# Attention and two expert stages on one core: a list scheduler with measured durations, a cost for changes of tile size, and constants fetched first

## The chip, the core and the metric

The kernel runs on one core of a Trainium2 chip. The metric is the device time of one execution in microseconds (us); lower is better. A core has five instruction streams that run side by side and wait for each other through semaphores: TensorE (PE, with its weight loads shown as PEld), VectorE (DVE), ScalarE (ACT), GpSimd (POOL) and SyncE (SP), which here issues all DMAs.

## What is computed

Float32 attention with a soft cap on the scores feeds a first expert stage, whose activation is a ratio of two polynomials, and a second one that takes the largest of three products:

```python
scores = cap * np.tanh((q @ k.T / sqrt(64)) / cap)          # 2 x 12 heads, 448 tokens, 64 wide
attn = softmax(scores); x = attn @ v                        # -> 896 tokens x 768
h = x @ w_in                                                # 768 -> 2048
P = a0 + a1*h + a2*h**2 + a3*h**3
Q = 1 + |b0|*|h| + |b1|*h**2
x = (P / (Q + 1e-6)) @ w_out                                # 2048 -> 768
y = max(x @ w1, x @ w2, x @ w3) @ w_out2                    # 768 -> 768
```

The weights arrive as 64-bit numbers and are decoded on the chip. Every product of the expert stages is made of three matmuls (high by high, high by low, low by high parts), so that float32 accuracy is kept.

## The kernel before

**Stages.** Attention goes by 6 groups `d` of 4 heads. For each, `scores(d, i)` (lines 481 to 519) makes 7 tiles of scores; ACT turns each into weights with a tanh (L512) and an exp (L515), both on 128x896. `weighted_rest` and `weighted` (L532, L551) multiply them with v, `summed` (L574) adds up the rows, and the sums go through DRAM and back to be spread over the partitions (`sums`, `comp`, `rsum`, `row`), after which x is scaled and split (L610 to L618). Then come 32 units `up(n)`, a 128-wide slice `fc` of w_in by one of two batches `b` each, of 18 matmuls of 128x448 (L638); two units make a pair `k`. ACT and DVE turn a pair's product into the ratio: abs and cubic read the PSUM bank on ACT (L655, L658), first and second on DVE (L669, L672), linear (L662, L664) and denom (L677) make the denominator, Ln and Exp on ACT (L693, L694) and newton, numer, refine on DVE (L697, L700, L703) the quotient, and L717, L720 split it into `gh` and `gl`. `down("oa", ...)` (L745) multiplies a pair with the first half of w_out's columns into six accumulators, 18 matmuls a pair; `down("ob", ...)` does the other half once all pairs are there. `branches` (L836) and `output` (L895) are the second expert stage. Between them runs the decoding of 56 weight blocks (L378 to L408), five passes over 128x768 and a subtraction, mostly on DVE.

**Order.** No engine's order is written by hand. `Flow.add` records each step with the engines that can do it and a duration for each; `Flow.issue` (lines 147 to 261) then simulates the core with these numbers, gives each free engine the ready step of least due time that fits into free slots and banks, and emits it. PE steps get due times from a running clock that is started at 6.0 (line 361); all others from their users. `place` picks PSUM banks: `av` values go to banks 4 and 5, `h` values to 6 and 7 while scores are still to come, and any of the 8 after that, the one that has been free longest. `port` (lines 135 to 145) refuses POOL a step where DVE will soon do one that shares its port with POOL.

**Waits.** The pools are opened with `reuse_waits="tile"`: a reader or writer of a tile waits for the accesses of that tile before it. The PSUM tiles `b0` to `b3` are two banks each (line 293), so that both banks of one tile share their waits. There are 12 matmuls of warm-up (`3 * WARM`, L358) on a zeroed tile at the start.

Of the kernel before, what the change touches and what calls it, by code (L numbers as in the profile page):

```python
# [18 lines left out]
P = 128  # L19
# [15 lines left out]
NFULL = S // P  # L35
WARM = 4
EARLY = 4

AHEAD, NEAR, LEAVE = 200.0, 30.0, 4

LATE, KEEP = 40.0, 4

SHARE = 0.5
# [10 lines left out]
class Op:  # L54
    def __init__(self, engines, after, vals, fn, shared, due, leave, ahead, size):
        self.engines, self.after, self.vals, self.fn = engines, after, vals, fn
        self.shared, self.due, self.leave, self.ahead, self.size = shared, due, leave, ahead, size
        self.next, self.soft, self.left, self.ready, self.done, self.on = [], [], 0, 0.0, None, None

# [5 lines left out]
class Flow:  # L65
# [10 lines left out]

    def add(self, engines, fn, after=(), vals=(), shared=False, due=None, leave=0, ahead=1e9, size=0.0):
        first = next(iter(engines))
        if first == "pe":
            due = self.clock  # L80
            self.clock += engines["pe"]
        after = [a for a in after if a is not None]
        op = Op(engines, after, list(dict.fromkeys(vals)), fn, shared, due, leave, ahead, size)
# [50 lines left out]

    def port(self, t, op, ready, busy, current):

        if busy["dve"] > t + 1e-9 and current["dve"].shared:
            return False
        room = max(0.0, busy["dve"] - t)
        for o in ready:  # L140
            if "dve" in o.engines and o is not op and o.ready <= t + 1e-9:
                if o.shared:
                    return room >= SHARE * op.engines["pool"]
                room += o.engines["dve"]
        return True

    def issue(self):
        ops = self.ops
        for op in reversed(ops):
            d = min(op.engines.values())  # L150
# [7 lines left out]
        busy = dict.fromkeys(names, 0.0)  # L158
        current = dict.fromkeys(names)
        wire, head, left = 0.0, 0, len(ops)  # L160
        ready, events, seq = [], [], 0
# [5 lines left out]
        while left:  # L167
# [4 lines left out]
            while moved:  # L172
                moved = False
                for e in names:
                    if busy[e] > t + 1e-9:
                        continue
                    blocked = set()
                    ahead = dict.fromkeys(names, 0.0)
                    for op in ready:
                        first = next(iter(op.engines))  # L180
                        cost = op.engines[first]
# [13 lines left out]
                        if op.shared and e == "dve" and busy["pool"] > t + 1e-9:  # L195
                            continue
                        if e == "pool" and not self.port(t, op, ready, busy, current):
                            continue
                        if e != first and op.engines[e] > max(0.0, busy[first] - t) + ahead[first] + cost:
                            ahead[first] += cost  # L200
                            continue
                        break
                    else:
                        continue
                    ready.remove(op)
                    for v in op.vals:
                        if v.at is None:
                            self.take(v)
                    dur = op.engines[e]
                    op.on = e  # L210
                    current[e] = op
# [57 lines left out]
def attention_moe(ctx: ExitStack, tc: tile.TileContext, qk, v, w_in, w_out, w123, w_out2, par, out):  # L269
# [53 lines left out]

    con_in = dma(lambda: con, lambda: par.broadcast_to([P, 8]), size=0.004, issue=0.3)
    idle = slot("idle", F32R)
# [33 lines left out]

    add({"pe": 2.4}, warm_up, [zero], [idle, warm])  # L360
    fl.clock = 6.0

# [118 lines left out]
    def scores(d, i):  # L481
# [13 lines left out]
        def ends(e):  # L495
# [9 lines left out]
        done = add(  # L505
            {"pe": 0.8}, products if whole_ else ends, [QK[pi][1] for pi in pis], [QK[pi][0] for pi in pis] + [t]
        )
# [8 lines left out]

        th = add({"act": 0.80}, soft, [done, scale_in], [t, x])
        last_tanh.append(th)
# [5 lines left out]
    def weighted_rest(d):  # L524
# [11 lines left out]

        done = add({"pe": 0.85}, products, [ex, got_v], [*o, x, vr])
        AV[d] = o, done
# [4 lines left out]
    def weighted(d, r):  # L543
        vr, got_v = VV[d]
        o, dep = AV[d][0][r], AV[d][1]
        for n in range(NFULL):
# [8 lines left out]

            dep = add({"pe": 0.76}, products, [ex, got_v, dep], [o, x, vr])
        xu, parts = XU[d]
# [4 lines left out]
    def summed(d):  # L562
        t, row, dep = Val("av", f"sm{d}"), Val("row", f"sr{d}"), None
        for n in range(NFULL + 1):
# [13 lines left out]

            dep = add({"pe": 0.76}, products, [x[1] for x in xs] + [filled, dep], [t] + [x[0] for x in xs])
        got = add(  # L580
# [44 lines left out]
    def up(n):  # L625
# [4 lines left out]
        for part in range(3):  # L630

            def products(e, part=part):
# [10 lines left out]
            dep = add(  # L643
                {"pe": 1.2}, products, [w.done, dep] + [x[1] for x in xs], [h, w.hi, w.lo] + [x[0] for x in xs],
            )
# [82 lines left out]
    def down(which, n, half):  # L728
# [4 lines left out]
        for o in range(3):  # L733
# [14 lines left out]

            users.append(add({"pe": 0.6}, products, [w.done, h_, l_], [a, w.hi, w.lo, hi, lo]))
            if half and len(users) == 1:  # L750
# [69 lines left out]
    def branches(oc, b):  # L820
# [6 lines left out]
        for lo, hi in ranges:  # L827
            for m in range(3):
                w, o = weights["m", oc, m], outs[m]

                def products(e, w=w, o=o, lo=lo, hi=hi):
# [7 lines left out]
                last[m] = add(  # L839
                    {"pe": 0.6 * (hi - lo)}, products, [w.done, last[m]] + [x[1] for x in xs],  # L840
                    [o, w.hi, w.lo] + [x[0] for x in xs],
# [37 lines left out]
    def output(t):  # L879
# [4 lines left out]
        for half in range(2):  # L884
# [3 lines left out]
            def products(e, o=o, ck=ck):  # L888
# [9 lines left out]
            done = add(  # L898
                {"pe": 18 * 0.171}, products, [w.done for w in ws] + [d for h in H3 for d in h[2]],
                [o] + [x for w in ws for x in (w.hi, w.lo)] + [x for h in H3 for x in h[:2]],  # L900
# [65 lines left out]
```

## Time and profile before

| | |
|---|---|
| three runs | 557.7, 554.9, 557.12 us; median 557.12 |
| profiled execution | 559.87 us |
| its span | 558.1 us |
| mean granted TensorE clock | 0.985 |
| busy PE / DVE / ACT / POOL | 521.8 / 355.5 / 289.5 / 56.7 us |
| matmuls recorded | 2640 |
| DMA | 58.36 MB, mean 105 GB/s |

The profiled execution is 2.75 us above the median of the runs. Busy times are averages over stages with different limits; the section of rows below cuts the span into stages. In a row of the timeline the columns are start, length, engine, line, operation, out<-in with partitions x elements and count, and in brackets the idle time before it and what ended it.

### The profile page before, as it was taken

To read this page: it belongs to the slowest core of one execution; us is meant where nothing else is said; L and a number is where in the kernel's file an instruction comes from. 1 tells how busy PE (TensorE), PEld (TensorE's weight loads), DVE (VectorE), ACT (ScalarE), POOL (GpSimd) and SP (SyncE) were. 2 spreads that over 40 slices of the span, in tenths; PEclk is the share of its full clock that TensorE was granted. 3 is DMA by queue.
4 is the path that set the end of the run, shared out by engine and by line. 5 is a ranking of instruction groups with operands and counts; after the bars stand their busy time and mean duration, and the time that the engine had idled before them with its cause. 6 is when DMAs were issued, how large, how long until landed. Compare 5 with 4: busy or idle time off the path is not lost.

```text
span 558.1 us, 6678 instructions
## 1 busy us (share of the span) xinstructions
PE 521.8 (93%) x2640; PEld 415.0 (74%) x2640; DVE 355.5 (64%) x490; ACT 289.5 (52%) x365; POOL 56.7 (10%) x52
## 2 busy tenths in 40 slices
PE   7999999899986988788789999999999999999996
PEld 4222224468875878677678999999999999999996
DVE  0326798789897878787678989998895236112000
ACT  4999888665776657454348774535362111001111
POOL 0210021100321221120121100002000000000000
PEclk9999999999997999899799999999999999999999
DMA  7692455425210001302010457785550000000121
GB/s 288 253 358 72 158 160 159 137 91 168 93 58 1 0 1 56 115 17 98 0 56 1 127 160 265 253 281 200 189 166 1 1 1 0 1 0 1 58 84 58
DMA packets 16447, 58.36 MB, mean 105 GB/s; under 512 B 3592, under 2 KB 6944, under 8 KB 16416
## 3 DMA queue, kind: packets, MB, share of 16 engines
q1 hardware_dynamic: 16416, 57.94, 30.5%
q8 instruction: 20, 0.33, 0.2%
q14 instruction: 11, 0.09, 0.1%
HBM read 55.10 MB, written 2.84 MB: 104 GB/s over the span
## 4 chain that ended last, share of the span: by engine, by line
PE 75%; DVE 11%; ACT 6%; DMA 4%; issue 1%; SPq 1%; ACTq 0%; DVEq 0%
PE b L836 24%; PE b L638 17%; PE b L745 14%; PE b L895 8%; PE b L493 4%; PE b L551 4%; PE b L574 3%; DVE W L669 3%; ACT W L658 3%; DVE W L672 3%; DMA row<-rsum 2%; ACT A L655 2%; DMA con<-in_par_dram 1%; SPq L321 1%; PE b L532 1%
## 5 line engine op out<-in xcount | busy, mean ns | idle before, releaser
L638 PE MATMUL b<-x,whin 128*128 128x448 f32 x384 | 114.9, 381 | 20.9 <-DVE W L672 16.9
L836 PE MATMUL b<-x,whm 128*128 128x448 f32 x432 | 122.7, 365 | 0.0
L638 PEld LDWEIGHTS b<-x,whin 128*128 128x128 f32 x384 | 72.8, 194 | 39.0 <-DVE W L672 18.9
L836 PEld LDWEIGHTS b<-x,whm 128*128 128x128 f32 x432 | 81.2, 188 | 6.4
L836 PE MATMUL b<-x,wlm 128*128 128x448 f32 x216 | 78.9, 365 | 0.0
L638 PE MATMUL b<-x,wlin 128*128 128x448 f32 x192 | 71.8, 374 | 0.0
L658 ACT ACTIVATE W<-b,con 128x448 f32<-128x448 f32 x32 | 22.8, 724 | 39.4 <-PE b L638 35.0
L512 ACT ACTIVATE e<-b,qscale 128x896 f32<-128x896 f32 x42 | 41.0, 1019 | 4.4 <-PE b L493 4.3
L836 PEld LDWEIGHTS b<-x,wlm 128*128 128x128 f32 x216 | 40.6, 188 | 3.2
L515 ACT ACTIVATE e<-e,con 128x896 f32<-128x896 f32 x42 | 42.0, 1050 | 0.0
L745 PE MATMUL b<-gl,whoa 128*128 128x448 f32 x96 | 36.4, 379 | 3.6 <-DVE gl L720 3.6
L638 PEld LDWEIGHTS b<-x,wlin 128*128 128x128 f32 x192 | 37.2, 194 | 3.2
L864 ACT CAST h3h<-t 128x448 fp32r<-128x448 f32 x9 | 5.1, 567 | 65.7 <-DVE t L859 65.7
L745 PE MATMUL b<-gh,whoa 128*128 128x448 f32 x96 | 36.1, 376 | 2.5 <-ACT gh L717 2.5
L669 DVE TENSOR_TENSOR W<-b,W 128x448 f32<-128x448 f32 x32 | 19.7, 622 | 27.4 <-ACT A L655 16.6
L493 PE MATMUL b<-qk 64*128 64x448 f32 x144 | 35.3, 583 | 2.0 <-ACT e L512 2.0
L745 PE MATMUL b<-gh,wloa 128*128 128x448 f32 x96 | 35.9, 374 | 0.0
L745 PE MATMUL b<-gh,whob 128*128 128x448 f32 x96 | 35.2, 366 | 0.0
L745 PE MATMUL b<-gh,wlob 128*128 128x448 f32 x96 | 35.1, 365 | 0.0
L745 PE MATMUL b<-gl,whob 128*128 128x448 f32 x96 | 35.1, 365 | 0.0
L677 POOL TENSOR_TENSOR T<-T,A 128x448 f32<-128x448 f32 x15 | 20.5, 1369 | 102.7 <-ACT T L662 75.6
L551 PE MATMUL b<-e,v 128*64 128x448 f32 x144 | 30.7, 551 | 0.0
(114 smaller groups left out, 905.3 us busy)
## 6 DMA issues: line engine op xcount, KB each, us to landing
raw<-in_w_out_dram SPq DMA_DIRECT2D x22, 768.0 KB, 4.2
raw<-in_w_dram SPq DMA_DIRECT2D x18, 768.0 KB, 4.4
raw<-in_w_in_dram SPq DMA_DIRECT2D x16, 768.0 KB, 5.7
qk<-in_qk_dram SPq DMA_DIRECT2D x12, 448.0 KB, 5.1
v<-in_v_dram SPq DMA_DIRECT2D x6, 448.0 KB, 8.6
row<-rsum SPq DMA_DIRECT2D x24, 112.0 KB, 3.5
out_dram<-ob SPq DMA_DIRECT2D x6, 384.0 KB, 2.8
out_dram<-ob SPq DMA_DIRECT2D x2, 192.0 KB
```

The costliest lines, as they stand in the source:

```text
L493: pe.matmul(pair(t)[:, j, :S], k[rr], q[rr], start=True, stop=True)
L512: act.activation(two(x), pair(t)[:, :, :S], AF.Tanh, scale=qscale)
L515: act.activation(two(x), two(x), AF.Exp, scale=cap)
L551: pe.matmul(bank(o)[j * D : j * D + D, :S], whole(vr, n, r, j), two(x)[:, j], start=False, stop=n == NFULL - 1,)
L574: pe.matmul(bank(t)[g, :S], ones[:, 0 if n < NFULL else 1 + r], two(xs[r][0])[:, j], start=n == 0, stop=n == NFULL, tile_position=(0, (2 * ...
L638: pe.matmul(bank(h)[:, :S], w_, x_, start=cc == 0 and i == 0, stop=cc == NCC - 1 and i == len(terms) - 1)
L658: act.activation(two(w_)[:, i], bank(h)[:, :S], AF.Identity, bias=a2, scale=a3)
L669: dve.tensor_tensor(out=two(w_)[:, i], in0=bank(h)[:, :S], in1=two(w_)[:, i], op=ALU.mult)
L677: engine[e].tensor_tensor(out=two(t_)[:, i], in0=two(t_)[:, i], in1=two(a_)[:, i], op=ALU.mult)
L745: pe.matmul(bank(a)[:, :S], w_, g_, start=count[half, o, b] == 1, stop=count[half, o, b] == 3 * NFC)
L836: pe.matmul(bank(o)[:, :S], w_, x_, start=cc == 0 and i == 0, stop=cc == NCC - 1 and i == 2)
L895: pe.matmul(bank(o)[:, :NH], h_, w_, start=i == 0, stop=i == len(terms) - 1)
```

## The change

The durations that the scheduler plans with are altered: a score, weighting or sum step on PE from 0.76 to 0.85 to `FULL` = 0.752, an up step from 1.2 to 6 x 0.203, a down step from 0.6 to 3 x 0.203, an output step from 18 x 0.171 to 18 x 0.1733, a tanh from 0.80 to 0.89, the warm-up from 2.4 to 3.6. Each PE step of the attention now has a `mode` (its tile shape), a change of mode costs `SWITCH` = 0.1 in the plan, and PE may take a later ready step of its present mode if that is due at most `SAME` = 3.0 after the first one. `port` no longer counts DVE steps that are held back for lack of slots or for being too early. SP holds back a transfer that is due more than 14.0 ahead while the planned wire is over 2.0 behind. The constants get a due time of -20, so that they are fetched first; the warm-up falls from 12 to 9 matmuls and the clock of due times starts at 4.5.

```diff
-WARM = 4
+WARM = 3
+BACKLOG = 14.0, 2.0
+SWITCH, SAME = 0.1, 3.0
+MM, MO, FULL = 0.203, 0.1733, 0.752
...
     def port(self, t, op, ready, busy, current, v0):
...
             if "dve" in o.engines and o is not op and o.ready <= t + 1e-9:
+                if not (o.due - v0 < o.ahead and self.fits(o, v0)):
+                    continue
...
+                    choice = None
                     for op in ready:
+                        if choice and (op.due > choice.due + SAME or "pe" not in op.engines or op.mode != mode):
+                            continue
...
+                        if e == "sp" and op.due - v0 > BACKLOG[0] and wire > t + BACKLOG[1]:
+                            continue
...
+                        if e == "pe" and SAME and op.mode != mode:
+                            choice = choice or op
+                            continue
+                        choice = op
                         break
...
                     dur = op.engines[e]
+                    if e == "pe":
+                        dur += SWITCH if mode != op.mode else 0.0
+                        mode = op.mode
...
-    con_in = dma(lambda: con, lambda: par.broadcast_to([P, 8]), size=0.004, issue=0.3)
+    con_in = dma(lambda: con, lambda: par.broadcast_to([P, 8]), size=0.004, issue=0.45, due=-20.0)
...
-    add({"pe": 2.4}, warm_up, [zero], [idle, warm])
-    fl.clock = 6.0
+    add({"pe": 3 * WARM * 0.4}, warm_up, [zero], [idle, warm])
+    fl.clock = 4.5
...
-            {"pe": 0.8}, products if whole_ else ends, [QK[pi][1] for pi in pis], [QK[pi][0] for pi in pis] + [t]
+            {"pe": FULL}, products if whole_ else ends, [QK[pi][1] for pi in pis], [QK[pi][0] for pi in pis] + [t],
+            mode="rows" if whole_ else "both",
...
-        th = add({"act": 0.80}, soft, [done, scale_in], [t, x])
+        th = add({"act": 0.89}, soft, [done, scale_in], [t, x])
...
-        done = add({"pe": 0.85}, products, [ex, got_v], [*o, x, vr])
+        done = add({"pe": FULL}, products, [ex, got_v], [*o, x, vr], mode="both")
...
-            dep = add({"pe": 0.76}, products, [ex, got_v, dep], [o, x, vr])
+            dep = add({"pe": FULL}, products, [ex, got_v, dep], [o, x, vr], mode="halves")
...
-                {"pe": 1.2}, products, [w.done, dep] + [x[1] for x in xs], [h, w.hi, w.lo] + [x[0] for x in xs],
+                {"pe": 6 * MM}, products, [w.done, dep] + [x[1] for x in xs], [h, w.hi, w.lo] + [x[0] for x in xs],
...
-            users.append(add({"pe": 0.6}, products, [w.done, h_, l_], [a, w.hi, w.lo, hi, lo]))
+            users.append(add({"pe": 3 * MM}, products, [w.done, h_, l_], [a, w.hi, w.lo, hi, lo]))
```

The lines of the new file are 22 to 25 higher: L321 becomes L343, L638 L663, L658 L683, L655 L680, L669 L694, L672 L697, L677 L702, L703 L728, L720 L745, L745 L770.

Since the planner's numbers decide every order, the order of the program moves almost everywhere. Three places matter below. The first is SP at the program's start (`con` is the constants, `qk` and `v` the attention's inputs by pair and group, `raw` the undecoded weights). Before:

```order
L321 DMA qk0_110<-in_qk_dram 128x896
L321 DMA qk1_112<-in_qk_dram 128x896
L321 DMA con_68<-in_par_dram 128x8
L321 DMA qk2_127<-in_qk_dram 128x896
L321 DMA qk3_129<-in_qk_dram 128x896
L321 DMA v0_131<-in_v_dram 128x896
L321 DMA qk4_133<-in_qk_dram 128x896
```

and now:

```order
L343 DMA con_68<-in_par_dram 128x8
L343 DMA qk0_111<-in_qk_dram 128x896
L343 DMA qk1_122<-in_qk_dram 128x896
L343 DMA qk2_124<-in_qk_dram 128x896
L343 DMA qk3_126<-in_qk_dram 128x896
L343 DMA v0_145<-in_v_dram 128x896
L343 DMA qk4_155<-in_qk_dram 128x896
```

The constants go ahead of the first two `qk`, and the first transfers of weights fall behind `v2`.

The second is PE around the end of the up pair `fc` = 13 and the start of the down steps of pair 10 (`b0` to `b3` are PSUM tiles, `x` the scaled attention result of batch and chunk, `whin` and `wlin` the parts of w_in, `whoa` and `wloa` those of w_out, `gh` and `gl` the parts of the activation). Before:

```order
L638 MATMUL b3_84<-x0_5_668,whin13_1566 128x448 x2
L638 MATMUL b3_84<-x0_5_668,wlin13_1585 128x448
L638 MATMUL b3_84<-x1_4_1037,whin13_1566 128x448 x2
L638 MATMUL b3_84<-x1_4_1037,wlin13_1585 128x448
L638 MATMUL b3_84<-x1_5_1046,whin13_1566 128x448 x2
L638 MATMUL b3_84<-x1_5_1046,wlin13_1585 128x448
L745 MATMUL b2_83<-gh10_1779,whoa5_1680 128x448 [waits Activation_49]
L745 MATMUL b2_83<-gl10_1797,whoa5_1680 128x448
L745 MATMUL b2_83<-gh10_1779,wloa5_1723 128x448
L745 MATMUL b2_83<-gh10_1779,whoa5_1680 128x448
L745 MATMUL b2_83<-gl10_1797,whoa5_1680 128x448
L745 MATMUL b2_83<-gh10_1779,wloa5_1723 128x448
```

and now:

```order
L663 MATMUL b3_84<-x0_5_646,whin13_1764 128x448 x2
L663 MATMUL b3_84<-x0_5_646,wlin13_1772 128x448
L663 MATMUL b0_81<-x1_4_1035,whin13_1764 128x448 x2
L663 MATMUL b0_81<-x1_4_1035,wlin13_1772 128x448
L663 MATMUL b0_81<-x1_5_1046,whin13_1764 128x448 x2
L663 MATMUL b0_81<-x1_5_1046,wlin13_1772 128x448
L770 MATMUL b2_83<-gh10_1781,whoa5_1839 128x448
L770 MATMUL b2_83<-gl10_1802,whoa5_1839 128x448
L770 MATMUL b2_83<-gh10_1781,wloa5_1842 128x448
L770 MATMUL b0_81<-gh10_1781,whoa5_1839 128x448 [waits Activation_49]
L770 MATMUL b0_81<-gl10_1802,whoa5_1839 128x448
L770 MATMUL b0_81<-gh10_1781,wloa5_1842 128x448
```

Both units of a pair were in the two banks of `b3`; now the first is in `b3` and the second in `b0`, each beside an accumulator of the down steps, and the second group of three down matmuls waits for ACT. At the end of the same 18 down matmuls there is now a wait for DVE ahead of the group in `b3`:

```order
L770 MATMUL b1_82<-gh10_1781,whoa5_1839 128x448
L770 MATMUL b1_82<-gl10_1802,whoa5_1839 128x448
L770 MATMUL b1_82<-gh10_1781,wloa5_1842 128x448
L770 MATMUL b3_84<-gh10_1781,whoa5_1839 128x448 [waits DVE_49]
L770 MATMUL b3_84<-gl10_1802,whoa5_1839 128x448
L770 MATMUL b3_84<-gh10_1781,wloa5_1842 128x448
L663 MATMUL b3_84<-x0_0_430,whin14_1850 128x448 x2
```

Before, the first wait for DVE stood at the first matmul of the next up pair, behind all 18.

The third is DVE at the last pair (`W15`, `T15`) and the activation of pair 14 (`dec`, `wl`, `wh` are blocks of weights in decoding). Before:

```order
L664 TENSOR_SCALAR T15_2122<-A15_2115,absb_69 128x448
L720 TENSOR_TENSOR gl14_2131<-W14_2015,gh14_2110 128x896
L677 TENSOR_TENSOR T15_2122<-T15_2122,A15_2115 128x448 x2
L669 TENSOR_TENSOR W15_2129<-b3_84,W15_2129 128x448 x2
L672 SCALAR_TENSOR_TENSOR W15_2129<-W15_2129,con_68,b3_84 128x448 x2
L393 SCALAR_TENSOR_TENSOR decob1_2079<-raw1_75,decob1_2079 128x768
L384 TENSOR_SCALAR decob2_2088<-decob2_2088 128x768
L419 CAST whob1_2182<-decob1_2079 128x768
L403 SCALAR_TENSOR_TENSOR decob2_2088<-raw2_76,decob2_2088 128x768
L697 SCALAR_TENSOR_TENSOR T15_2122<-T15_2122,qone_72,A15_2115 128x896
L700 SCALAR_TENSOR_TENSOR W15_2129<-W15_2129,con_68,A15_2115 128x896
L408 TENSOR_TENSOR wlob1_2202<-decob1_2079,whob1_2182 128x768
```

and now:

```order
L689 TENSOR_SCALAR T15_2115<-A15_2111,absb_69 128x448
L406 TENSOR_SCALAR decob1_2089<-decob1_2089 128x768
L702 TENSOR_TENSOR T15_2115<-T15_2115,A15_2111 128x448
L694 TENSOR_TENSOR W15_2113<-b3_84,W15_2113 128x448
L689 TENSOR_SCALAR T15_2115<-A15_2111,absb_69 128x448
L745 TENSOR_TENSOR gl14_2138<-W14_2021,gh14_2120 128x896
L702 TENSOR_TENSOR T15_2115<-T15_2115,A15_2111 128x448
L694 TENSOR_TENSOR W15_2113<-b0_81,W15_2113 128x448
L697 SCALAR_TENSOR_TENSOR W15_2113<-W15_2113,con_68,b3_84 128x448
L697 SCALAR_TENSOR_TENSOR W15_2113<-W15_2113,con_68,b0_81 128x448
L415 SCALAR_TENSOR_TENSOR decob1_2089<-raw1_75,decob1_2089 128x768
L722 SCALAR_TENSOR_TENSOR T15_2115<-T15_2115,qone_72,A15_2111 128x896
```

The low part of pair 14 (`gl14`) stood ahead of pair 15's first and second; now it stands between them, and the four readers of the banks go in the order first, first, second, second, by bank.

## Rows read from the trace of the kernel before

**Rows 1.** Windows: window, length, busy us (count) by engine, granted clock, DMA share, GB/s.

```profile
14.00:56.00 42.00, 42.00 (x246) 11.49 (x246) 17.69 (x24) 40.94 (x46) 6.62 (x7) 1.00 0.61 227
56.00:98.00 42.00, 40.71 (x244) 13.01 (x240) 35.26 (x58) 36.72 (x41) 5.43 (x5) 1.00 0.51 159
101.00:171.20 70.20, 61.76 (x315) 48.14 (x311) 61.37 (x86) 46.78 (x63) 12.85 (x10) 0.99 0.31 100
171.20:320.30 149.10, 130.53 (x596) 116.33 (x597) 118.91 (x149) 86.13 (x112) 26.54 (x17) 0.95 0.13 44
305.20:558.10 252.90, 248.26 (x1261) 232.81 (x1259) 136.09 (x192) 82.56 (x109) 6.21 (x4) 1.00 0.30 102
```

**Rows 2.** Timeline of PE and ACT over the first 15 us.

```profile
1.38 4.61 PE L358 MATMUL b<-idle 128*128 128x448 f32 x12 [1.38 <-DVE idle L326]
5.91 1.77 PE L493 MATMUL b<-qk 64*128 64x448 f32 x8
10.58 3.72 PE L493 MATMUL b<-qk 64*128 64x448 f32 x16 [1.98 <-ACT e L512]
...
9.52 6.40 ACT L512 ACTIVATE e<-b,qscale 128x896 f32<-128x896 f32 x7
```

**Rows 3.** The chain that ended last, in order of time: start, length, what.

```profile
1.64 7.40 DMA con<-in_par_dram
...
25.22 0.90 PE b L551 x4
...
53.16 4.66 PE b L551 x24
...
187.28 7.58 PE b L638 x36
...
297.84 7.53 PE b L638 x36
```

**Rows 4.** Timeline of PE: a matmul that waited in the loop of up and down.

```profile
171.23 0.74 PE L745 MATMUL b<-gl,whoa 128*128 128x448 f32 x1 [3.10 <-DVE gl L720]
```

**Rows 5.** Window right behind this wait.

```profile
171.20:174.00 2.80, 2.77 (x7) 2.48 (x8) 2.01 (x3) 2.11 (x4) 1.59 (x1) 0.50 0.00 0
```

**Rows 6.** Timeline of one handover from an up pair to the next.

```profile
206.05 0.36 PE L638 MATMUL b<-x,wlin 128*128 128x448 f32 x1
...
206.53 1.15 DVE L697 SCALAR_TENSOR_TENSOR T<-T,qone,A 128x896 f32<-128x896 f32 x1
...
207.26 0.36 PE L638 MATMUL b<-x,wlin 128*128 128x448 f32 x1
...
207.66 0.72 ACT L658 ACTIVATE W<-b,con 128x448 f32<-128x448 f32 x1 [1.39 <-PE b L638]
...
208.29 0.54 ACT L655 ACTIVATE A<-b 128x448 f32<-128x448 f32 x1
...
208.86 0.62 DVE L669 TENSOR_TENSOR W<-b,W 128x448 f32<-128x448 f32 x1 [1.18 <-ACT A L655]
...
209.40 1.14 DVE L700 SCALAR_TENSOR_TENSOR W<-W,con,A 128x896 f32<-128x896 f32 x1
...
209.52 0.73 ACT L658 ACTIVATE W<-b,con 128x448 f32<-128x448 f32 x1 [0.69 <-DVE W L669]
...
211.96 0.68 DVE L672 SCALAR_TENSOR_TENSOR W<-W,con,b 128x448 f32<-128x448 f32 x1
...
212.70 0.67 PE L638 MATMUL b<-x,whin 128*128 128x448 f32 x2 [1.42 <-DVE W L672]
```

**Rows 7.** Timeline of DVE at the end of the loop.

```profile
315.96 0.95 DVE L408 TENSOR_TENSOR wlob<-decob,whob 128x768 fp32r<-128x768 f32 x1
316.83 1.09 DVE L703 SCALAR_TENSOR_TENSOR W<-T,W 128x896 f32<-128x896 f32 x1
...
319.17 1.09 DVE L720 TENSOR_TENSOR gl<-W,gh 128x896 fp32r<-128x896 f32 x1
```

More of the change, by code (lines that the diff above doesn't have):

```diff
@@ L54, with __init__ @@
 class Op:
-    def __init__(self, engines, after, vals, fn, shared, due, leave, ahead, size):
+    def __init__(self, engines, after, vals, fn, shared, due, leave, ahead, size, mode):
         self.engines, self.after, self.vals, self.fn = engines, after, vals, fn
         self.shared, self.due, self.leave, self.ahead, self.size = shared, due, leave, ahead, size
+        self.mode = mode
         self.next, self.soft, self.left, self.ready, self.done, self.on = [], [], 0, 0.0, None, None
@@ L75, in __init__, with add @@
         self.banks, self.freed, self.log = [None] * 8, [0.0] * 8, []
-    def add(self, engines, fn, after=(), vals=(), shared=False, due=None, leave=0, ahead=1e9, size=0.0):
+    def add(self, engines, fn, after=(), vals=(), shared=False, due=None, leave=0, ahead=1e9, size=0.0, mode=None):
         first = next(iter(engines))
@@ L82, in add @@
         after = [a for a in after if a is not None]
-        op = Op(engines, after, list(dict.fromkeys(vals)), fn, shared, due, leave, ahead, size)
+        op = Op(engines, after, list(dict.fromkeys(vals)), fn, shared, due, leave, ahead, size, mode)
         for v in op.vals:
@@ L133, in fits, with port @@
         return True
-    def port(self, t, op, ready, busy, current):
+    def port(self, t, op, ready, busy, current, v0):
         if busy["dve"] > t + 1e-9 and current["dve"].shared:
@@ L159, in issue @@
         current = dict.fromkeys(names)
+        mode = None
         wire, head, left = 0.0, 0, len(ops)
@@ L196, in issue @@
                             continue
-                        if e == "pool" and not self.port(t, op, ready, busy, current):
+                        if e == "sp" and op.due - v0 > BACKLOG[0] and wire > t + BACKLOG[1]:
+                            continue
+                        if e == "pool" and not self.port(t, op, ready, busy, current, v0):
                             continue
@@ L201, in issue @@
                             continue
+                        if e == "pe" and SAME and op.mode != mode:
+                            choice = choice or op
+                            continue
+                        choice = op
                         break
-                    else:
+                    if choice is None:
                         continue
+                    op = choice
                     ready.remove(op)
@@ L577, in products @@
                         )
-            dep = add({"pe": 0.76}, products, [x[1] for x in xs] + [filled, dep], [t] + [x[0] for x in xs])
+            dep = add(
+                {"pe": FULL}, products, [x[1] for x in xs] + [filled, dep], [t] + [x[0] for x in xs], mode="quarters",
+            )
         got = add(
@@ L839, in branches @@
                 last[m] = add(
-                    {"pe": 0.6 * (hi - lo)}, products, [w.done, last[m]] + [x[1] for x in xs],
+                    {"pe": 3 * MM * (hi - lo)}, products, [w.done, last[m]] + [x[1] for x in xs],
                     [o, w.hi, w.lo] + [x[0] for x in xs],
@@ L898, in output @@
             done = add(
-                {"pe": 18 * 0.171}, products, [w.done for w in ws] + [d for h in H3 for d in h[2]],
+                {"pe": 18 * MO}, products, [w.done for w in ws] + [d for h in H3 for d in h[2]],
                 [o] + [x for w in ws for x in (w.hi, w.lo)] + [x for h in H3 for x in h[:2]],
```

## The prediction, made before the changed kernel ran

> **What bounds the kernel now.** I read the windows first, then the chain of waits, then the timeline of PE, DVE and ACT where the chain changes hands. The reader should see four stages. From 14 to 56 us PE is busy 42.00 of 42.00 us and ACT 40.94; from 56 to 98 us PE is busy 40.71 and ACT 36.72 [rows 1]: attention is bound by PE, with ACT close behind. From 101 us to 320 us no engine is full: DVE leads with 61.37 of 70.20 us (87%) and then 118.91 of 149.10 us (80%), and PE loses 18.6 us of the second window. From 305.2 us to the end PE is busy 248.26 of 252.90 us, most of the rest being gaps in the records, and nothing can be won there. So time can be won at the start, a little in attention, and in the loop of up and down steps.
>
> At the start PE works 4.61 us at the warm-up, then at scores, and then stands 1.98 us for the first tanh, which starts at 9.52 [rows 2]. The chain of waits begins with the constants, which are issued third at 1.64 and take 7.40 us, so that they are there at 9.04 [rows 3]. The tanh needs them.
>
> In the loop the chain has eight handovers between the pair of up units that starts at 187.28 and the one that starts at 297.84 [rows 3], 13.8 us each. The pace of PE is six matmuls between 206.05 and 207.26 [rows 6], 0.202 each, so the 54 matmuls of a handover are 10.9 us of work and 2.9 us are lost. One handover shows how: the last matmul of the pair ends at 207.62 (207.26 and 0.36); the next pair begins at 212.70, 5.08 us later, while the 18 down matmuls between them take 3.64. ACT's cubic of the *first* unit starts only at 207.66, although that unit was complete six matmuls before: both units lie in one PSUM tile. ACT and DVE then take turns until DVE's second at 211.96 lets the pair begin [rows 6]. After an idle time of 3.10 us [rows 4] the granted clock was 0.50 (the 1.2 GHz level) for 2.8 us [rows 5], which costs another 1.4 us; the window's mean of 0.95 [rows 1] says that there is more of it.
>
> **The start.** The constants are issued ahead of `qk0`, and the warm-up has 9 matmuls. At 4.61 / 12 = 0.384 us each, PE is free 1.16 us earlier, at 4.75. The tanh no longer waits for the constants but for the first scores, so the stop of 1.98 us goes as well: 3.1 us at most, if the inputs are in time. `qk0` and `qk1` are now queued one transfer later; I take 0.3 us for that. **-2.8, bounds -3.1 to 0** (0 if ACT, 97% busy in the first window, cannot follow, or the clock does not, below). The first weights fall behind `v2` on SP and their decoding starts later: nothing, because DVE has 24 us free from 14 to 56 us [rows 1]; without that cover a late transfer would stop the first up steps.
>
> **Changes of tile size.** A weighting step alone takes 0.90 us, six in a row 4.66 [rows 3]: 0.75 each and 0.15 for the change. Counted on PE's order there are 91 changes up to the last attention step before and 84 now: 7 x 0.15, **-1.0, bounds -1.0 to 0**, since ACT has just 1.06 us to spare in the first window [rows 1].
>
> **The loop.** Two ways give its size. *By the handover:* the units now lie in `b3` and `b0`. With the pair's end as 0, ACT's cubic of the first unit can run from -1.2 to -0.45 (0.72), its abs to 0.1 (0.54), the second unit's cubic to 0.85 (0.73) [rows 6]. The down group in `b0` has its turn at 0.61 and waits 0.25 for that. ACT's abs of `b0` then waits for this group (to 1.5) and ends at 2.05, DVE's first at 2.7 and the second of `b3` at 3.35 (0.62, 0.68), just when the last group, in `b3`, has its turn; that is a wait of 0.1. The next pair begins at 4.0 instead of 5.08: -1.05, eight times -8.4, and with two such stretches at half clock less about -11. For this DVE's numer, which now stands ahead of these, must start 1.75 us before the pair's end. If it starts at 0.05, when newton ended before (206.53 and 1.15, [rows 6], less 207.62), the second of `b3` ends at 5.2 and the loss is 2.1 us instead of 2.9: about -7. *By DVE:* counted on its order, between `gl2` and `gl15` there are 145 instructions for 148, fewer of the passes over weights and more of denom (of which POOL now does 8 and not 15), which by the rows' durations is 2.6 us less: 116.3 for 118.9. At the 80% of this window and with the 3 us that DVE does more ahead of `gl2` nothing is won; at the 87% of the window before, 116.3 / 0.874 = 133 us, -16. The middle, 83.6%, gives 139.1 us, -10. I take **-9, bounds -16 to 0**, the middle of -11 and -7 by the handover, to which -10 is near.
>
> **The transition.** When the last up pair ended at 305.37 (297.84 and 7.53, [rows 3]) PE had 78 matmuls that did not need `gl15`: 54 for pairs 12 to 14 and 24 of the second half; these last until 321.1, and `gl15` was ready at 320.26 [rows 7]. Now only 12 of the second half stand there: 12 x 0.202 = 2.4 us less cover, 0.8 of it spare: **+1.6, bounds 0 to +3.5** (`gl14` moves behind pair 15's first, and new waits of PE on the banks come up to 1.1 us).
>
> **The sum.** -2.8 - 1.0 - 9 + 1.6 = -11.2 against the profiled 559.87 us: 548.7. The three runs' median is 2.75 us below the profiled execution, so the forecast for the runs is **545.9 us**. About 0.5%, 2.8 us, is what a measurement of this kernel can tell from no change.
>
> **Rivals.**
>
> *DVE sets the pace, and nothing is won.* If DVE's 80% is not the result of waits for banks but its own chain (Ln, Exp and newton to refine follow each other), the loop stays as long as it is, and what the start gains is waited for again at 101 us, where DVE is 87% busy. For it: that number, and seven denoms that POOL gives up. Against it: the 1.18 us in which DVE waits for ACT in the handover [rows 6]. About 557 us.
>
> *Slower: the banks shared with accumulators stop PE twice.* Before, one wait for DVE stood behind all 18 down matmuls; now one stands ahead of the last three. DVE's order there is numer (1.14), refine, a subtraction of weights, first, first, second: 1.14 + 1.09 + 0.95 + 2 x 0.62 + 0.68 = 5.1 us [rows 6, 7]. If numer starts 1.8 us behind the pair's end, as it did before (209.40), the group in `b3` can start only at 6.9 while its turn is 3.3; with 0.25 for `b0` and about 0.7 for a half clock after an idle time over 3 us, 4.6 us are lost in a handover instead of 2.9. Eight times 1.7 is +14 in place of -9: about 569 us. It decides where numer starts more than 0.85 us behind the pair's end: 0.85 + 5.1 - 3.3 + 0.25 is the 2.9 of before. For it: the planner sees banks one by one in `place`, while waits go by tiles. Against it: before, numer stood behind a first that waited for ACT [rows 6], and now it does not.
>
> *The clock.* The first scores after the warm-up of 4.61 us took 1.77 us for 8 matmuls, and the warm-up's own were 0.384 apart, against 0.202 in the loop [rows 2, 6]. If 3.5 us of warm-up leave the scores at the slower pace, their 2.7 us are doubled, and the start's gain is lost: about 548.6 us. The Trainium skill ("TensorE: Matmul & The Clock Gate", "Part 1: The HAM clock gate (the "warmup" mystery)") says that the array runs at half rate until it has been busy for a sustained while, and that when this ends varies from run to run, which speaks against any shortening of a warm-up; that the matmuls of the warm-up were at about half the pace agrees with it, and no run here shows a shorter one.
>
> *PE at its floor.* If the banks were all that held PE, a loss of 0.4 us stays in each handover: 8 x 2.5 = -20 in the loop, and about 535 us.
>
> For the start there is also a rule against the new order. The first group of rows 2 shows only that the constants were late, not why. The Trainium skill ("DMA: Bandwidth & Descriptors", "Specifications") asks for transfers of at least 512 bytes for the full rate, and the constants are 32 bytes for each partition; by it they could hold up `qk0` behind them, and an estimate from rows of what that would cost at most is the 1.2 us that the shorter warm-up saves. The sum would then be 547.1.
>
> **How the numbers follow.** The forecast has 0.57, no gain 0.15, the two stops 0.14, the clock 0.08, the floor 0.06. Faster by over 0.5% is forecast, clock and floor: 0.71; within 0.5%: 0.15; slower: 0.14. The bounds of the terms give 537 for a loop of -16 with a forecast otherwise, and 557 for one of 0; the range 537 to 559 leaves out the two stops and half of the floor, 0.17 of the chance.
>
> **What would show it.** *Start:* the first tanh at about 5.3 us, no stop of PE before 15 us, attention's end 3 to 4 us earlier. *Loop:* up pairs 12.3 to 13.0 us apart, ACT's cubic in the last six matmuls of a pair, and no window at clock 0.50. *Two stops:* waits over 3 us at the third-last down matmul, put down to DVE's second, with windows at 0.50 behind them. *No gain:* DVE at 80% and pairs 13.8 apart. *Transition:* a wait for `gl15` of about 1.6 us. The prediction is wrong if the loop takes 110 us or more for eight handovers, or if attention ends no earlier.

## The result and the profile after

The changed kernel took 537.0 us (median of 4 runs, 535.87 to 539.05), against 556.01 us before (median of 4): a ratio of 0.967, with a 95% interval of 0.961 to 0.972. The forecast was 545.9 us with a range from 537.0 to 559.0, so the time lies on the range's lower end. The profiled execution took 537.27 us with a span of 535.5 us, 22.6 us less than the 559.87 and 558.1 us of before.

The windows of the changed kernel, with the columns of [rows 1] and cut at the same places of the program, but for the fourth, which begins 1.0 us before the end of `gl2` (166.23):

```profile
12.00:54.00 42.00, 42.00 (x254) 11.80 (x248) 23.44 (x31) 41.15 (x47) 6.59 (x6) 1.00 0.68 255
54.00:96.00 42.00, 40.15 (x240) 13.67 (x237) 36.21 (x55) 37.87 (x41) 6.44 (x7) 1.00 0.56 190
99.00:165.20 66.20, 61.22 (x298) 46.16 (x299) 57.31 (x82) 43.35 (x56) 14.14 (x10) 0.97 0.35 112
165.20:295.60 130.40, 125.42 (x602) 111.63 (x601) 115.47 (x148) 89.84 (x119) 16.55 (x9) 1.00 0.09 31
281.70:535.50 253.80, 249.00 (x1262) 232.57 (x1260) 133.50 (x185) 86.25 (x111) 6.54 (x5) 1.00 0.29 98
```

The first two and the last are nearly as before. Most of the time went in the fourth, from `gl2` to `gl15`: 130.4 us instead of 149.1 (129.4 from the end of `gl2`). DVE is busy 89% of it, not 80%, and the granted clock is 1.00 throughout. PE's idle time there fell from 18.57 to 4.98 us. A matmul takes 125.42 / 602 = 0.208 us of PE's busy time instead of 130.53 / 596 = 0.219, which for some 600 of them is 6.4 us more. That is about what the half clock cost, which is gone now: before, it came in three stretches, the first of which goes on from [rows 5] (windows of the kernel before):

```profile
174.00:177.00 3.00, 3.00 (x11) 2.52 (x10) 3.00 (x5) 2.30 (x3) 0.00 (x0) 0.63 0.01 3
226.90:229.00 2.10, 2.10 (x7) 1.89 (x8) 1.74 (x2) 2.07 (x3) 0.00 (x0) 0.62 0.00 0
229.00:231.00 2.00, 2.00 (x7) 1.78 (x6) 2.00 (x4) 1.99 (x2) 0.00 (x0) 0.54 0.44 80
269.50:272.00 2.50, 2.50 (x7) 2.24 (x8) 0.48 (x1) 1.90 (x2) 0.00 (x0) 0.50 0.00 0
272.00:274.00 2.00, 2.00 (x7) 1.78 (x6) 1.82 (x2) 0.82 (x2) 0.00 (x0) 0.50 0.00 0
274.00:277.00 3.00, 3.00 (x13) 2.71 (x13) 2.97 (x3) 0.00 (x0) 1.62 (x1) 0.80 0.00 0
```

The missing share of the clock times the length of each window, with [rows 5], adds up to 7.1 us.

What PE waited for from 165 to 300 us, by the view of lines (busy, mean ns of one, idle time before, releasers), first in the kernel before:

```profile
L638 PE MATMUL b<-x,whin 128*128 128x448 f32 x212 | 64.6, 387 | 18.5 <-DVE W L672 15.3 <-DVE W L669 2.0 <-ACT A L655 1.2
```

and in the changed one:

```profile
L663 PE MATMUL b<-x,whin 128*128 128x448 f32 x238 | 67.9, 366 | 0.0
L770 PE MATMUL b<-gh,whoa 128*128 128x448 f32 x84 | 32.0, 381 | 5.0 <-ACT W L683 1.9 <-ACT A L680 1.4 <-DVE W L697 1.2
```

No up step waits any more here. The new waits, of down groups for ACT and DVE, are there as the order showed, but cost 5.0 us in all. One handover of the changed kernel, the answer to [rows 6] (timeline of PE, ACT and DVE):

```profile
245.52 0.36 PE L663 MATMUL b<-x,wlin 128*128 128x448 f32 x1
...
246.93 0.47 PE L770 MATMUL b<-gh,whoa 128*128 128x448 f32 x1 [0.44 <-ACT W L683]
...
250.48 0.57 PE L663 MATMUL b<-x,whin 128*128 128x448 f32 x2
...
245.54 1.34 ACT L683 ACTIVATE W<-b,con 128x448 f32<-128x448 f32 x2
...
249.16 0.98 ACT L680 ACTIVATE A<-b 128x448 f32<-128x448 f32 x2 [1.45 <-DVE W L697]
...
247.91 0.62 DVE L694 TENSOR_TENSOR W<-b,W 128x448 f32<-128x448 f32 x1 [0.93 <-PE b L770]
...
250.17 0.68 DVE L697 SCALAR_TENSOR_TENSOR W<-W,con,b 128x448 f32<-128x448 f32 x1 [1.05 <-ACT A L680]
```

The pair ends at 245.88 (245.52 and 0.36) and the next begins at 250.48, 4.60 us later, with the 0.44 us for ACT on `b0` in it. In this handover the second of `b0` runs at 250.17 and holds up nothing: it reads `b0`, while the next pair's first unit goes to `b3`.

The start, by the timeline of PE and of ACT:

```profile
1.37 3.73 PE L380 MATMUL b<-idle 128*128 128x448 f32 x9 [1.37 <-DVE idle L348]
5.10 1.77 PE L515 MATMUL b<-qk 64*128 64x448 f32 x8
...
7.71 4.13 PE L515 MATMUL b<-qk 64*128 64x448 f32 x20
...
6.17 6.41 ACT L535 ACTIVATE e<-b,qscale 128x896 f32<-128x896 f32 x7 [1.95 <-PE b L515]
```

The stop at 10.58 [rows 2] is gone and the first tanh starts at 6.17 instead of 9.52. The scores behind 9 matmuls of warm-up ran at the pace of before (1.77 us for 8). The last exp of attention, before and now, by the timeline of ACT:

```profile
94.93 1.03 ACT L515 ACTIVATE e<-e,con 128x896 f32<-128x896 f32 x1
...
92.93 1.05 ACT L538 ACTIVATE e<-e,con 128x896 f32<-128x896 f32 x1
```

It ends at 93.98 instead of 95.96.

### The profile page after: what moved, and what is told of

Its sections match the earlier page's. It is cut to its first block, busy times and chain, and to the rows that moved or that the text cites. A ratio compares the mean times of both kernels' runs of the same rounds, so it can differ in the third digit from the quotient of the medians.

```text
span 535.5 us, 6669 instructions
## 1 busy us (share of the span) xinstructions
PE 516.2 (96%) x2637; PEld 409.5 (76%) x2637; DVE 354.7 (66%) x485; ACT 299.1 (56%) x376; POOL 51.6 (10%) x46
## 4 chain that ended last, share of the span: by engine, by line
PE 73%; DVE 14%; ACT 6%; DMA 3%; issue 2%; SPq 1%; DVEq 0%; ACTq 0%
PE b L861 25%; PE b L770 17%; PE b L663 10%; PE b L920 8%; PE b L515 5%; PE b L597 3%; PE b L574 3%; DVE W L697 2%; DMA row<-rsum 2%; DVE T L722 1%; ACT A L680 1%; DVE W L694 1%; DVE W L725 1%; ACT W L683 1%; DVE T L702 1%
## 5 line engine op out<-in xcount | busy, mean ns | idle before, releaser
L663 PE MATMUL b<-x,whin 128*128 128x448 f32 x384 | 111.5, 372 | 5.2 <-DVE W L697 5.0
L663 PEld LDWEIGHTS b<-x,whin 128*128 128x128 f32 x384 | 71.2, 189 | 21.0 <-DVE W L697 7.3
L663 PE MATMUL b<-x,wlin 128*128 128x448 f32 x192 | 70.6, 368 | 0.0
L770 PE MATMUL b<-gh,whoa 128*128 128x448 f32 x96 | 36.5, 380 | 5.3 <-ACT W L683 1.9
L663 PEld LDWEIGHTS b<-x,wlin 128*128 128x128 f32 x192 | 36.2, 189 | 3.1
L889 ACT CAST h3h<-t 128x448 fp32r<-128x448 f32 x11 | 6.2, 567 | 57.2 <-DVE t L884 57.2
L770 PE MATMUL b<-gh,whob 128*128 128x448 f32 x96 | 35.3, 367 | 1.1 <-DVE x L789 1.1
L770 PE MATMUL b<-gl,whoa 128*128 128x448 f32 x96 | 35.2, 367 | 0.9 <-DVE gl L745 0.9
L683 ACT ACTIVATE W<-b,con 128x448 f32<-128x448 f32 x32 | 23.0, 724 | 22.0 <-PE b L663 19.7
L770 PE MATMUL b<-gh,wloa 128*128 128x448 f32 x96 | 35.1, 366 | 0.0
L770 PE MATMUL b<-gh,wlob 128*128 128x448 f32 x96 | 35.1, 365 | 0.0
L770 PE MATMUL b<-gl,whob 128*128 128x448 f32 x96 | 35.0, 365 | 0.0
L422 ACT ACTIVATE raw<-raw 128x768 uint8<-128x768 uint8 x16 | 31.5, 1972 | 2.0 <-POOL deco L402 1.7
L879 DVE TENSOR_TENSOR t<-b,t 128x448 f32<-128x448 f32 x12 | 7.5, 624 | 36.2 <-PE b L861 23.3
```

Source lines behind the costliest of these rows:

```text
L422: act.activation(byte[:, 4::8], byte[:, 3::8], AF.Copy, scale=1 / 32, bias=-31 / 64)
L663: pe.matmul(bank(h)[:, :S], w_, x_, start=cc == 0 and i == 0, stop=cc == NCC - 1 and i == len(terms) - 1)
L683: act.activation(two(w_)[:, i], bank(h)[:, :S], AF.Identity, bias=a2, scale=a3)
L770: pe.matmul(bank(a)[:, :S], w_, g_, start=count[half, o, b] == 1, stop=count[half, o, b] == 3 * NFC)
```

## The experiments

The theory after the result was that the placement of the two units of a pair in different PSUM tiles makes the gain, and not the durations and rules themselves. The rivals: the new order on DVE and ACT, the start, and the rules taken one by one. Ratios are to runs of the kernel before on the same chip, taken together with them; medians of different rows can come from different chips.

| kernel | edit | ratio, 95% interval | median us |
|---|---|---|---|
| the change | | 0.967, 0.961 to 0.972 | 537.0 |
| b_split | before, pair in two tiles, orders unchanged | 1.044, 1.038 to 1.050 | 583.1 |
| b_split2 | the same, up units alone | 0.968, 0.966 to 0.971 | 540.5 |
| b_start | before, with the new start | 0.995, 0.991 to 1.000 | 553.7 |
| a_same | change, pair in one tile | 0.983, 0.979 to 0.988 | 549.1 |
| a_nosw | change, without tile-size rule | 0.999, 0.995 to 1.003 | 557.6 |
| b_one | before, a tile for each unit | 0.956, 0.953 to 0.958 | 533.2 |
| a_one | change, a tile for each unit | 0.956, 0.952 to 0.961 | 534.0 |
| b_one_start | b_one, with the new start | 0.945, 0.938 to 0.952 | 527.3 |
| a_one_noport | a_one, old rule for POOL | 0.959, 0.953 to 0.965 | 534.2 |
| a_one_nosw | a_one, without tile-size rule | 0.960, 0.954 to 0.965 | 535.8 |
| a_one_nodur | a_one, old durations | 0.951, 0.946 to 0.956 | 530.9 |
| a_warm3 | change, 3 matmuls of warm-up | 0.969, 0.965 to 0.974 | 541.1 |

**b_split: the banks alone.** Which free bank a value gets changes nothing in the plan once the scores are done, so the placement can be changed with every engine's order kept. The edit acts from the first pairs on:

```diff
+LIKE = {"acc0": (2, 3, 4, 5, 6, 7), "h": (0, 1)}
...
-        return min(order, key=lambda at: max(self.freed[i] for i in at)) if order else None
+        like = LIKE.get(v.name[:4] if v.kind == "acc" else v.kind, ())
+        return min(order, key=lambda at: (at[0] not in like, max(self.freed[i] for i in at))) if order else None
```

> The kernel before, with every engine's order of instructions unchanged; only the choice among free PSUM banks differs, so that from the pair fc = 6 on the two units of a pair lie in the tiles b3 and b1, each beside an accumulator, and no longer both in b3. Theory 'banks': the loop's gain is the split, so up pairs come 11.5 to 12.5 us apart instead of 13.8, and the run takes 538 to 545 us. Rival 'order': the gain comes from the new order on DVE and ACT and from which engine does denom; then at most 3 us are won here, 553 us or more. Rival 'two stops': the sharing with accumulators alone costs time, 560 us or more.

It took 583.1 us, outside what the theory said and as the third rival had it, but not for its reason. Windows of the loop from the ninth pair (fc = 8) to the last, and of the second expert stage:

```profile
195.00:277.40 82.40, 79.05 (x380) 70.33 (x380) 75.96 (x93) 50.79 (x69) 17.28 (x12) 1.00 0.17 58
359.90:523.40 163.50, 139.96 (x649) 119.07 (x647) 67.54 (x100) 34.26 (x45) 3.51 (x2) 1.00 0.13 45
```

The same seven pairs take 97.7 us in the kernel before:

```profile
200.10:297.80 97.70, 83.26 (x378) 73.82 (x378) 74.89 (x93) 50.48 (x67) 16.64 (x12) 0.95 0.14 49
```

The loop is 15.3 us shorter, with the order of before. The loss lies behind it. The second stage's products and the output are of kind `h` as well, so that the edit reached further than meant and drew them all into one tile, where PE waited for the steps that read the products out (groups of b_split's page):

```profile
L840 PE MATMUL b<-x,whm 128*128 128x448 f32 x432 | 126.0, 373 | 22.1 <-DVE t L858 7.5
...
L899 PE MATMUL b<-who,h3h 128*128 128x384 f32 x84 | 29.5, 351 | 8.3 <-ACT ob L910 6.8
```

**b_split2: the same for the up units alone.** The preference for banks 0 and 1 asks for names that begin with h, which only up units have.

```diff
+        like = ()
+        if v.name.startswith("acc0"):
+            like = (2, 3, 4, 5, 6, 7)
+        elif v.kind == "h" and v.name[0] == "h":
+            like = (0, 1)
```

> As b_split, the kernel before with every engine's order unchanged and the two units of a pair in b3 and b1, but the preference for banks 0 and 1 is given to the up units alone and no longer to the products of the second expert stage. Theory 'banks': the loop is that of b_split (pairs 11.7 us apart, second stage begun at 358 to 362 us), the second stage's waits of PE (30 us in b_split) go, and the run takes 536 to 541 us. Rival: the 30 us there came from the split itself, 580 us or more.

It took 540.5 us, 0.968: with not one instruction moved, the placement gives what the whole change gives. Windows as for b_split:

```profile
193.20:275.40 82.20, 78.98 (x380) 70.32 (x379) 75.89 (x93) 50.72 (x69) 17.22 (x12) 1.00 0.17 58
357.00:489.20 132.20, 131.52 (x649) 121.55 (x648) 66.75 (x100) 34.42 (x45) 3.57 (x2) 1.00 0.16 55
```

**a_same: the change with a pair in one tile.**

```diff
-            order = [(4,), (5,)] if v.kind == "av" else [(i,) for i in range(8)]
+            order = [(4,), (5,)] if v.kind == "av" else [(i,) for i in (ACC if v.name.startswith("acc0") else range(8))]
```

with `ACC = 0, 1, 2, 3, 4, 5`.

> The changed kernel with the first half's accumulators kept to banks 0 to 5, so that from the pair fc = 7 on both units lie in b3 again; the planner's order differs from there on in places. Theory 'banks': pairs come 13.5 us apart again and the run takes 549 to 556 us. Rival 'order': the new order keeps its gain, 535 to 541 us.

It took 549.1 us: the seven pairs take 89.8 us instead of the 81.9 of the change, 12.8 us apart where 13.5 was expected. The plan's order differs in places, so that this bounds the placement less sharply than b_split2. The 0.983 says that the change's order and start give something without the placement: the seven pairs are 7.9 us shorter than the 97.7 of before, and the clock stays at 1.00. The two don't add up: b_split2, with the order of before, already gains as much as the whole change.

```profile
195.30:285.10 89.80, 78.75 (x379) 70.33 (x379) 70.38 (x90) 55.03 (x73) 10.63 (x6) 1.00 0.10 36
```

**a_nosw: the change without the rule on tile sizes** (`SWITCH, SAME = 0.0, 0.0`). Its plan happens to put both units into `b3`.

> The changed kernel without the cost of a change of tile size in the plan and without the choice of a later step of the same size (SWITCH and SAME at 0). The plan that comes out puts both units of a pair into b3 from fc = 6 on. Theory 'banks': pairs are 12.8 to 13.8 us apart and the run takes 547 to 556 us, although the edit concerns attention alone. Rival 'tile sizes': only the changes of tile size come back, 7 x 0.15 us, 537 to 539 us.

It took 557.6 us, 0.999: the edit concerns attention, which ends no later (92.25 us, against 93.98 in the change); most of the loss is in the loop, 94.2 us for the seven pairs at a granted clock of 0.96.

```profile
192.90:287.10 94.20, 82.78 (x379) 72.88 (x379) 73.86 (x92) 47.30 (x66) 13.10 (x9) 0.96 0.12 42
```

**b_start: the new start alone** (the `con` transfer, `WARM` and the clock of 4.5 as in the change; the planner's order moves with them).

> The kernel before with only the constants fetched first, 9 matmuls of warm-up and the clock of due times at 4.5; both units of a pair stay in b3. Theory: the first tanh ends 3.4 us earlier, as in the changed kernel, PE has no stop before 15 us, and 1 to 3.4 us of it reach the end: 552.5 to 555 us. Rival 'swallowed': DVE is 87% busy after attention and the gain is waited for there: 556 us, the same. Rival 'clock': the scores behind 9 matmuls run at half the pace and nothing is gained at the first tanh.

The ratio is 0.995, at the edge of what can be told. PE has no stop before 15 us, but the first scores took 2.50 us and not 1.77:

```profile
5.11 2.50 PE L493 MATMUL b<-qk 64*128 64x448 f32 x8
```

**a_warm3: a still shorter warm-up**, plan and orders unchanged:

```diff
-        for _ in range(3 * WARM):
+        for _ in range(3):
```

> The changed kernel, plan and orders unchanged, with 3 matmuls of warm-up in place of 9. Theory: the first scores run at half the pace (8 of them in 3.3 to 3.6 us and not 1.77), PE starts them at the landing of the first inputs, and the whole is within 1.5 us of 537. Rival: the pace of the scores has nothing to do with the warm-up, 1.77 us again.

```profile
1.38 1.49 PE L380 MATMUL b<-idle 128*128 128x448 f32 x3 [1.38 <-DVE idle L348]
5.11 3.36 PE L515 MATMUL b<-qk 64*128 64x448 f32 x8 [2.25 <-DMA qk<-in_qk_dram]
8.40 1.41 PE L522 MATMUL b<-qk 64*64 64x448 f32 x8
```

The first scores run at about half the pace, as expected. The two runs gave 539.75 and 542.44 us, more than the 1.5 us around 537 that were expected, but beside the kernel before of the same chip that is 0.969, which can't be told from the change's 0.967: what the shorter warm-up costs the whole stays open.

**b_one and a_one: a tile for each unit.** Scores use the bank pairs 0 and 1, 2 and 3, 6 and 7, so that banks 4 and 5 can be tiles of their own. With the accumulators kept to the other six, the up units of the loop (from fc = 7 in both) have a tile each and share waits with nobody:

```diff
+ACC = 0, 1, 2, 3, 6, 7
...
-            order = [(4,), (5,)] if v.kind == "av" else [(i,) for i in range(8)]
+            order = [(4,), (5,)] if v.kind == "av" else [(i,) for i in (ACC if v.name.startswith("acc0") else range(8))]
...
-    twos = [pp.tile([P, 2, 512], F32, name=f"b{i}") for i in range(4)]
+    twos = {i: pp.tile([P, 2, 512], F32, name=f"b{i}") for i in (0, 1, 3)}
+    ones_ = {i: pp.tile([P, 512], F32, name=f"c{i}") for i in (4, 5)}
...
-        return twos[val.at[0] // 2][:, val.at[0] % 2]
+        i = val.at[0]
+        return ones_[i] if i in ones_ else twos[i // 2][:, i % 2]
```

> The changed kernel with banks 4 and 5 as tiles of their own (scores never use them) and the first half's accumulators kept to the other six banks, so that from fc = 6 on each unit of a pair has a tile to itself and shares waits with no accumulator. Theory 'banks': the 0.8 us that PE still loses in a handover are partly waits on shared tiles (ACT for the second group, DVE for the last); 2 to 5 us are won, 532 to 535 us. Rival 'DVE': DVE is 88% busy in the loop and sets the pace, 536 to 538 us.

> The kernel before with banks 4 and 5 as tiles of their own and the up units of the loop in them, as in a_one; durations, order rules and the start are those of before. Theory 'banks': the loop needs nothing else of the change, so pairs are 11.0 to 11.8 us apart and the run takes 534 to 539 us, behind a_one (534.0) by no more than the start and the tile sizes are worth, 1 to 4 us. Rival 'order': the old order of DVE and ACT keeps the pairs 13 us or more apart, 548 us or more.

Both take 0.956. The planner's order moves in places in both, but in b_one every duration, every rule of order and the start are those of before. It was expected 1 to 4 us behind a_one and is not. In the old kernel with these tiles PE is busy 78.08 of the 78.10 us of the seven pairs:

```profile
190.90:269.00 78.10, 78.08 (x379) 70.82 (x378) 72.24 (x91) 51.00 (x69) 16.17 (x10) 1.00 0.21 71
```

So the loop of before needed none of the change's durations, rules or start, only tiles.

**b_one_start.** The edits of b_one and b_start together.

> b_one with the constants fetched first, 9 matmuls of warm-up and the clock of due times at 4.5. Theory: with the loop free of shared tiles, what b_start won (0.5%) adds up, ratio 0.949 to 0.953, about 530.5 us. Rival: the gain is waited for behind attention, or lost at a half clock in the first scores, ratio 0.954 to 0.958 as b_one.

The ratio is 0.945, 527.3 us: the fastest kernel of the study, faster than both given ones. That fits a loop bound by PE, behind which an earlier start reaches the end. It is more than the expected 0.949 to 0.953 and than b_start's 0.5%, but 0.956 x 0.995 = 0.951 lies inside its interval.

**What the other rules are worth beside it.** a_one has the new start and all the other edits and is slower than b_one_start. Three runs undo one edit of a_one each: POOL's rule (the two added lines of `port` out), the tile sizes, the durations (0.8, 0.85, 0.76, 0.80 for the tanh, steps of 0.2 and 0.171).

> a_one with POOL refused again for steps of DVE that are held back. Theory: with the banks out of the way the rule moves two denoms between engines and is worth nothing, ratio 0.954 to 0.959. Rival: DVE is 88% busy in the loop, so what POOL takes or leaves there is seen, over 0.5% either way.

> a_one with SWITCH and SAME at 0; both units of a pair have tiles of their own from fc = 7 on. Theory 'banks': what a_nosw lost (3%) was the placement alone; with tiles of their own it is not lost, ratio 0.945 to 0.959. Rival 'tile sizes': without the rule the loss stays, 0.97 or more. If b_one_start's lead over a_one (0.945 to 0.956) is due to this rule, the ratio is 0.945 to 0.949; if not, 0.955 to 0.958.

> a_one with the durations of before in the plan. Theory: they are worth nothing once the banks are out of the way, ratio 0.953 to 0.959. If b_one_start's lead over a_one is due to the new durations, 0.945 to 0.949; if the new durations help, 0.962 or more.

Without the rule on tile sizes a_nosw had lost the whole gain; with a tile for each unit nothing is lost (0.960 beside 0.956). POOL's rule is worth nothing that shows (0.959). With the old durations the kernel is at 0.951, between a_one and b_one_start, with intervals that overlap both. Why a_one stands behind b_one_start isn't settled, but the profiles show where. The spans are 6.9 us apart (532.2 and 525.3). Attention's last exp ends at 93.63 in a_one and at 89.51 in b_one_start (89.86 in b_start), and behind the last up pair PE waits 1.6 us in a_one and not at all in b_one_start or a_one_nodur. With one edit undone attention ends at 93.25 (POOL's rule), 91.91 (tile sizes) and 92.56 (durations), so none of the three accounts for it alone. These are single executions. The four with the attention of before (before, b_split, b_split2, b_one) end it between 93.41 and 96.48, so that a difference of 4.1 us stands out and those under 3 us don't. The limit on SP and pairs of edits weren't tried.

## Why the prediction was right, and where it was off

**Reading of before: right.** The up units' shared tile was what PE waited for, DVE was not the limit at 80%, and the tail gave nothing (131.3 us of second stage in both).

**Start, -2.8, and tile sizes, -1.0: the mechanism of the start right, the sizes not met.** The end of the last exp moved by 2.0 us (95.96 to 93.98), where the sum of both terms was 3.8 and the sign to look for 3 to 4; the first tanh came at 6.17 and not at 5.3. Even the 2.0 are not clear of chance: the four executions with the attention of before end it between 93.41 and 96.48, the three with that of the change (the change, a_same, a_one) between 93.63 and 95.83. The end of `gl2` moved by 4.9 (171.17 to 166.23), but 2.9 of these arose behind attention, where the units of a pair lie in different tiles from fc = 4 on: they belong to the placement or the order and not to these terms. Of the 1.0 for tile sizes nothing shows: without that rule attention ended at 92.25 (a_nosw) and 91.91 (a_one_nosw), with it at 93.98 and 93.63. With the new start and the old durations and rules it ended at 89.86 (b_start) and 89.51 (b_one_start), a gain beyond the start's term, about 4 us of which the change's other edits gave up. The stop in [rows 2] was itself unusually long: in three other executions with the start of before (b_split, b_split2, b_one) the constants landed 5.2, 5.4 and 5.7 us after their issue and not 7.40, and the first tanh began at 7.32, 7.54 and 7.79 and not at 9.52. In b_split:

```profile
1.64 5.21 DMA con<-in_par_dram
```

**Loop, -9, bounds -16 to 0: the mechanism right, the size off.** From `gl2` to `gl15` 149.1 us became 130.4, and by the ends of the two (320.26 to 295.64) the difference is -19.7 us, outside the bounds. The pairs came 11.7 us apart, not 12.3 to 13.0. The step that failed is the one that took the handover at 206 to 213 us for all eight. It lost 1.4 us, while the mean of the eight was 2.9, which stood in the same text; -1.05 times eight could only give the smaller half. The half clock was counted at two stretches of 1.4 us each, 2.8 us; there were three and longer ones, 6.4 us by the busy time of a matmul and 7.1 by the windows. Idle time gave the other 13.6. The handover by hand of 4.0 us was nearly met: by the starts of PE's pairs, the seven from fc = 8 on are 81.9 / 7 = 11.7 us apart, 0.8 us over their work. The use of DVE, for which I took 83.6% as a middle, was a result and not a limit: with tiles of their own PE is full, and DVE is busy 72.24 of 78.10 us (92%).

**Transition, +1.6: the wait did not come.** The second expert stage begins 21.5 us earlier (378.26 to 356.76) where `gl15` came 24.6 earlier: +3.1, inside the bounds, but `gl15` is no measure of PE, as fewer matmuls stand ahead of it. From the end of the last up pair (305.37 and 281.90) to the second stage PE took 74.9 us instead of 72.9, +2.0, and no wait for `gl15` is in it. What PE waited for, 1.3 us in all, was DVE's first (0.2) and DVE's step that reads the down products out (1.1).

**The sum.** -4.9 - 19.7 + 3.1 is -21.5; another 1.1 us lies behind the last matmul, at the end of the output. The profiled execution of before was 3.9 us above the median of its runs, that of the change 0.3, so that the medians differ by 19.0. That the time lies in the range is luck. The terms' lower bounds add up to -20.1 us and the profiled spans differ by 22.6; and with the rest as forecast the prediction's sum gives 538.9 for a loop of -16 and 554.9 for one of 0, where it wrote 537 and 557. Only this slip of 2 us holds the 537.0.

**The rivals.** *PE at its floor* (0.06, about 535 us) came nearest; it was the forecast with the idle time counted right. *No gain by DVE* fell, as b_one's busy DVE shows. *Two stops* fell in the loop: the waits on the shared banks cost 5.0 us in all, and those for DVE 1.2 of them. That sharing does cost is what b_one against b_split2 says (0.956 and 0.968, with some difference in order), and the place where it stopped PE at each step was the second stage of b_split. *The clock* did not decide in the change's profile, but that was one execution: of the nine kernels profiled with 9 matmuls of warm-up only the change ran its first 8 scores in 1.77 us, and the other eight took 2.04 to 2.79; behind 12 matmuls all four took 1.77, and behind 3 it was 3.36 (a_warm3). The granted clock reads 1.00 in the rows of the start, so that the pace alone shows this. The Trainium skill ("TensorE: Matmul & The Clock Gate", "Part 1: The HAM clock gate (the "warmup" mystery)") has the array at half rate until it has been busy for a sustained while, with the end varying from run to run; these profiles agree with it.

**The small transfer ahead of the inputs.** The first `qk` landed at 3.87 us before and at 5.05 in the change, 0.45 us of it for the later issue. That cost little, as the 9 matmuls end at 5.10; in a_warm3 PE waited for it until 5.11. The Trainium skill ("DMA: Bandwidth & Descriptors", "Specifications") has transfers under 512 bytes below the full rate, which would fit the other 0.7 us; that their size is the reason, no run here shows.

## What to carry to other kernels

When a planner's numbers change, look at what else its choices move: here a choice among equally free banks, which no cost in the plan knows, was worth as much as the whole change. Waits go by the tile, so give each value that is filled, read and refilled on its own rhythm a tile of its own, and test this with the orders kept. Price a loop by the mean loss of its rounds, not by the round that is easiest to follow, and look for the same stop in other executions before you count on removing it.

## What the runs showed of the hardware

The half clock made idle time dearer than it looks: in the window of [rows 1] the 18.57 us of idle time came with 6.4 us of slower matmuls, and most of both went when the waits did. The landing of the 4 KB of constants took 7.40, 5.2, 5.4 and 5.7 us from issue in four executions with the same queue order at the start, a spread of 2.2 us, where the start was forecast to win 2.8. Behind 9 matmuls of warm-up (3.73 us) the first 8 scores took between 1.77 and 2.79 us, behind 12 (4.32 to 4.61 us) always 1.77.
